# Router logits in narrow column tiles, rows of twelve groups turned by VectorE from a copy in DRAM

## The chip, the cores and the metric

One core of one Trainium2 chip. The metric is the device time of one execution in microseconds (us), the median of several runs. PE is TensorE, PEld its weight load, DVE is VectorE, ACT is ScalarE, POOL is GpSimd, SP is SyncE, whose queue issues most of the DMAs.

## The reference: what is computed

Three layers over 2304 tokens of 512 features, all in f32. Attention over 4 batches x 8 heads keeps the 32 largest scores of each row; a gated feed-forward layer (512 to 2048 to 512) follows; a router then gives each token to one of 8 experts (512 to 1024 to 512), weighted with a softmax probability. The change lies at the router's logits:

```python
xn = x / (np.linalg.norm(x, axis=-1, keepdims=True) + 1e-06)
en = expert_emb / (np.linalg.norm(expert_emb, axis=-1, keepdims=True) + 1e-06)
logits = xn @ en.T / tau
expert_idx = np.argmax(logits, axis=1)
```

## The kernel before, in words

The tokens form 18 groups of 128. A written-out loop of 76 steps handles 72 attention units; `step` (line 840) runs the names of one of four lists (FIRST, MID, THEN, ODD) in that order, so the program order on every engine is the order of the list. From step 21 on, even steps use THEN and odd steps ODD. An attention unit passes through five steps: scores (PE, `scores`), their copy (ACT, `take`), sorted halves and the top 32 (DVE, `pairs` and `select`), mask (ACT, POOL), exponent (ACT), scaling (POOL), nine transposes (PE, `turned`, line 521), and `values` (PE, line 539).

Two groups at a time go through the feed-forward layer (`push_group`), as eight items of one step each: `s1` (24 matmuls, line 603), `gate` (ACT), `swish` (DVE), `large` (ACT), `small` (POOL), and one step later `s2` (12 matmuls, line 638). After the eighth item `out_y` copies each group's rows from PSUM to SBUF (`ysb`, line 649), stores them to `y_dram` (line 650), and calls `route`.

`route` appends work to the list `side`. Each step pops one entry of it, at the name `aside`. Before the change a group has two entries. `r1`: ACT squares the row and sums it into `ss_all` (line 666), PE transposes four blocks (line 669), ACT copies them out (line 671). `r2`: four f32 matmuls with the transposed row as the 128 x 128 weights and 8 columns of the embedding `ent` moving (line 677; an f32 matmul is two instructions in the trace), then a DVE copy into `l_all` (line 678). After groups 3, 7, 11 and 13, `choose` and `rank` (which expert, which place) follow in the same list. Pairs of groups 0-1 to 14-15 go this way, eight pairs; the last pair of groups 16-17 is handled behind the loop (lines 1130 to 1145), where its eight transposes stand at line 1133.

Behind the loop, `behind` (line 1060) pops the last entries of `side` at fixed places between the remaining feed-forward items; then come the experts, which gather rows from `y_dram`.

PSUM banks of `bank()` alternate between two; `turned`, `r1` and `r2` share them. `ps_sc`, the bank pair of the scores, has one buffer: the scores of the next unit wait until DVE's `pairs` has read the last. The SBUF pool `stg` has three buffers of 4 KB a partition; the weights' preparation uses it up to step 20, `ysb` after that.

Of the kernel before, what the change touches and what calls it, by code (L numbers as in the profile page):

```python
# [8 lines left out]
F32 = mybir.dt.float32  # L9
# [4 lines left out]
AF = mybir.ActivationFunctionType  # L14
ALU = mybir.AluOpType
AX = mybir.AxisListType
# [4 lines left out]
DM, FF = 512, 2048  # L21
E, F2 = 8, 1024
# [7 lines left out]

TURNS = (0, 1, 2, 3, 4, 6, 7, 5)
ACROSS = (2, 3)
NEG = -3.0e38
BIG = 2.0 ** 100
NUNIT = 72
# [24 lines left out]
def fused_kernel(tc: tile.TileContext, *args):  # L60

    nc = tc.nc
    y_dram = tc.dram_tile([NT + 1, DM], F32, name="y_dram")
    g_dram = tc.dram_tile([NT + 128, 1], F32, name="g_dram")
    tbl = tc.dram_tile([E * STRIDE, 2], I32, name="tbl")

    lo_dram = [tc.dram_tile([8, 128, 1024], F32, name=f"lo_dram{n}") for n in range(2)]
    with ExitStack() as held:  # L70
        pools = [held.enter_context(tc.tile_pool(name=n, bufs=b, **kw)) for n, b, kw in
                 (("const", 1, {}), ("sm", 4, {}), ("fs", 1, {}), ("ps_a", 1, {"space": PSUM}))]
        flag = pools[0].tile([1, 2], I32, name="flag")
        consts = {}
        over_ = layers(tc, *args, y_dram, g_dram, tbl, lo_dram, flag, pools, consts)
        rare = nc.values_load(flag[0:1, 1:2], min_val=0, max_val=NT + 1)  # L76
        with tc.If(rare > 0):
            over_()
            again = nc.values_load(flag[0:1, 0:1], min_val=0, max_val=1)
            with tc.If(again > 0):  # L80
                layers(tc, *args, y_dram, g_dram, tbl, lo_dram, None, pools, consts)()


class Held:
# [7 lines left out]
        return self.tiles[name]  # L92


def layers(tc: tile.TileContext, qt, kt, v, w_in, w_out, embt, tau, w1, w2, out, y_dram, g_dram, tbl, lo_dram, flag, pools, consts):
    nc = tc.nc
    exact = flag is None

    const = Held(pools[0], consts)
    sm, fs, ps_a = pools[1:]  # L100
    ident = const.tile([128, 128], F32, name="ident")
    half = const.tile([128, 1], F32, name="half")
    iota8 = const.tile([128, 8], F32, name="iota8")
    ebase = const.tile([128, 8], F32, name="ebase")
    ones = const.tile([128, 128], BF16, name="ones")
    tri = const.tile([128, 128], BF16, name="tri")
    ids = const.tile([128, NG, 2], I32, name="ids")
    ent = const.tile([128, 4, E], F32, name="ent")
    picks = const.tile([128, NG, E], BF16, name="picks")
    before = const.tile([128, NG + 1, E], BF16, name="before")  # L110
    rev8 = const.tile([128, 8], F32, name="rev8")
# [2 lines left out]
    l_all = const.tile([128, NG, E], F32, name="l_all")  # L114
    ss_all = const.tile([128, NG], F32, name="ss_all")
# [4 lines left out]
    st = ExitStack()  # L120
# [4 lines left out]
    mp = st.enter_context(tc.tile_pool(name="mp", bufs=2))  # L125
    lop = st.enter_context(tc.tile_pool(name="lop", bufs=2))
    stg = st.enter_context(tc.tile_pool(name="stg", bufs=3))
# [8 lines left out]
    def bank():  # L136
        turn[1] ^= 1
        return bank_t[turn[1]]

    def half_a():  # L140
        turn[0] ^= 1
        return bank_a[:, turn[0], :]
# [11 lines left out]
    emb = {}  # L154

    def embed(part):

        if part == 0:
            emb["et"] = fs.tile([128, 4, E], F32, tag="df", name="et")
            nc.sync.dma_start(out=emb["et"], in_=embt.rearrange("(k p) e -> p k e", p=128))  # L160
            emb["tb"] = fs.tile([128, 1], F32, tag="gt", name="tb")
            nc.sync.dma_start(out=emb["tb"], in_=tau.rearrange("(o t) -> o t", o=1).broadcast_to([128, 1]))
        elif part == 1:
            emb["ones"] = mp.tile([128, DM], F32, tag="wf", name="onesf", bufs=4)[:, :128]
            nc.gpsimd.memset(emb["ones"], 1.0)
            emb["sq"] = fs.tile([128, 4, E], F32, tag="tmp", name="sq")
            nc.scalar.activation(emb["sq"], emb["et"], AF.Square)
        elif part == 2:
            onesf, sq = emb["ones"], emb["sq"]
            emb["pe"] = pe = half_a()  # L170
            for k in range(4):
                nc.tensor.matmul(pe[:, :E], onesf, sq[:, k, :], start=(k == 0), stop=(k == 3))
        elif part == 3:
            emb["nr"] = fs.tile([128, E], F32, tag="nrm", name="nr")
            nc.scalar.activation(emb["nr"], emb["pe"][:, :E], AF.Sqrt)
        else:
            nr = emb["nr"]
            nc.vector.tensor_scalar(nr, nr, 1e-6, emb["tb"][:, 0:1], op0=ALU.add, op1=ALU.mult)
            nc.vector.reciprocal(nr, nr)
            nc.vector.tensor_tensor(ent, emb["et"], nr.unsqueeze(1).broadcast_to([128, 4, E]), op=ALU.mult)  # L180
# [24 lines left out]
    for q in range(8):  # L205
        c = slice(256 * q, 256 * q + 256)
# [250 lines left out]
    def select(i, r):  # L457
# [13 lines left out]
        if r < TOPK // 8 - 1:  # L471
            for n in range(2):
                nc.vector.match_replace(dst[:, n, :w], A[:, n, 8 * r:8 * r + 8], src[:, n, :w], NEG)

# [101 lines left out]
    side = deque()  # L576
    step = [0]

    done_groups, scored, chosen = [0], [0], [0]
# [4 lines left out]
    def push_group(X, gs):  # L584
# [3 lines left out]
        state = {}  # L588
# [56 lines left out]

        def out_y(o):
            final = gs[o] >= NG - 2
            t = late["xg"].tile([128, DM], F32, tag="xg", name="ysl") if final else stg.tile([128, DM], F32, tag="st", name="ysb")
            nc.scalar.copy(t, state["y"][o])
            nc.sync.dma_start(out=y_dram[128 * gs[o]:128 * gs[o] + 128, :], in_=t)  # L650
            if final:
                finals.append((t, gs[o]))
            else:
                route(t, gs[o])

        for q in range(8):
            moe.append((q, s1, gate, swish, large, small, s2, len(gs)))
# [2 lines left out]

    def route(ysb, g):
        state = {}

        def r1():
            sq = mp.tile([128, DM], F32, tag="wf", name="sqy", bufs=4)
            nc.scalar.activation(sq, ysb, AF.Square, accum_out=ss_all[:, g:g + 1])
            pp = bank()
            for k in range(4):
                nc.tensor.transpose(pp[:, 128 * k:128 * k + 128], ysb[:, 128 * k:128 * k + 128], ident)
            yt = mp.tile([128, DM], F32, tag="ug", name="yt", bufs=1).rearrange("p (k n) -> p k n", k=4)  # L670
            nc.scalar.copy(yt, pp.rearrange("p (k n) -> p k n", k=4))
            state["yt"] = yt

        def r2():
            p2 = bank()[:, :E]
            for k in range(4):
                nc.tensor.matmul(p2, state["yt"][:, k, :], ent[:, k, :], start=(k == 0), stop=(k == 3))
            nc.vector.tensor_copy(l_all[:, g, :], p2)
            scored[0] += 1

        side.extend((r1, r2))
        if g in (3, 7, 11, 13):
            side.extend((choose, rank))

    open_ = deque()
# [55 lines left out]
    late = {}  # L741
# [150 lines left out]
    if True:  # L892
# [17 lines left out]
        def hidden(r, f, c0, c1, half=None):  # L910
            xh_, xl_ = tok[r]
            h1, l1 = ws1[r]
            if r not in hs:
                hs[r] = [hp.tile([128, 8, CAPS[0]], F32R, tag=t, name=t) for t in ("hh", "hl")]
            if half != 1:
                xt_[f] = late["ph"].tile([128, 512], F32, tag="ph", name="ph2")[:, :c1 - c0]
            ph = xt_[f]
            for k in ((0, 1), (2, 3), (0, 1, 2, 3))[2 if half is None else half]:
                for n, (l, x) in enumerate(((h1, xh_), (h1, xl_), (l1, xh_))):
                    nc.tensor.matmul(ph, l[:, k, 128 * f:128 * f + 128], x[:, k, c0:c1], start=(k == 0 and n == 0), stop=(k == 3 and n == 2))  # L920
# [37 lines left out]
        def columns(r, d):  # L958
# [3 lines left out]
            if d == 0:  # L962
                across[r] = gp.tile([128, 4, CAPS[ACROSS[0]]], F32, tag="ot", name="ot", bufs=1)
            po = po_.tile([128, DM], F32, tag="po", name="po4")[:, :m]
# [135 lines left out]
        with tc.manual_schedule():  # L1100
# [29 lines left out]
            for o, (t, g) in enumerate(finals):  # L1130
                pp = px.tile([128, 4, 128], F32, tag="px", name="pxt")
                for k in range(4):
                    nc.tensor.transpose(pp[:, k, :], t[:, 128 * k:128 * k + 128], ident)
                yts.append(gp.tile([128, 4, 128], F32, tag="ob", name="ytl"))
                nc.scalar.copy(yts[o], pp)
                hidden(0, 1, *C, o)
            hidden_out(0, 0, *C)
            p2 = half_a()
# [47 lines left out]
            def leave(r, b):  # L1186
                rows_out(r, b)
                if ahead_:
                    gates(*ahead_.popleft())

            back = deque()
            for r, then, nn in zip(TURNS, TURNS[1:] + (None,), TURNS[2:] + (None, None)):
# [16 lines left out]
                if nn is not None:  # L1209
                    load2(nn)  # L1210
                    for x in bl[nn]:
                        get(nn, x)
                for n, b in enumerate(b2 if r not in ACROSS else range(4)):
                    if r in ACROSS:
                        columns(r, n)
# [4 lines left out]
                    if n == 0 and then is not None:  # L1220
                        for k in range(4):
                            split_1(then, k)
                        if nn is not None:
                            load1(nn)
                    if r not in ACROSS:
                        leave(r, b)
                if r in ACROSS:
                    back.extend((r, b) for b in b2)
# [95 lines left out]
```

## Time and profile before

| | us |
|---|---|
| median of 3 runs | 1027.08 (1026.25 to 1028.41) |
| the profiled execution | 1029.51 |
| its span, first to last instruction | 1027.8 |
| PE busy in the span | 953.9 |
| DVE busy | 760.3 |
| ACT busy | 715.1 |
| POOL busy | 632.0 |

The profile is of one execution, 2.4 us above the median. Busy time of PE includes the fill of the pipeline, so a busy share of 100% doesn't by itself mean matmuls back to back; distances between starts do. In a view of groups a row has the line, engine, operation, tiles, shapes and count, then the busy time and the mean duration of one in ns, then the idle time before and what ended it.

### The profile page before, as it was taken

The numbers are of one execution on the slowest core, as the hardware profiler recorded it, in microseconds if no ns is written. First come the engines' busy times: TensorE is split into PE (matmuls) and PEld (weight loads), VectorE is DVE, ScalarE is ACT, GpSimd is POOL, SyncE is SP. The second block draws the span as 40 slices with busy tenths as digits, with TensorE's granted clock in tenths as the row PEclk, the third lists the DMA queues.
The fourth block names the chain that finished last, engine by engine and source line by source line (L and its number), as shares of the span: only waits on it lengthen the run. The fifth ranks groups of instructions, "written<-read, shape, count | busy, mean of one in ns | idle before, by whom it ended". The sixth has DMA issues, their size and how long they took to land. (4 is left out here: it accounts for less than half of the span.)

```text
span 1027.8 us, 20958 instructions
## 1 busy us (share of the span) xinstructions
PE 953.9 (93%) x7268; PEld 842.0 (82%) x7268; DVE 760.3 (74%) x2349; ACT 715.1 (70%) x1445; POOL 632.0 (61%) x786
## 2 busy tenths in 40 slices
PE   3665787999999999999999999999999999999997
PEld 1443566889999899999999988789898888999996
DVE  7999999998988988988988888881234454555550
ACT  4899798897888787788787786775234453455551
POOL 4789899877778877778877665765232253034320
PEclk9956799999999999999999999999999999999999
DMA  5555678644445653456654275575586466445610
GB/s 199 178 158 176 223 238 270 216 159 141 140 140 173 206 177 118 114 173 179 183 168 143 81 246 198 138 240 197 164 254 218 130 228 216 169 147 195 253 75 22
DMA packets 85905, 180.96 MB, mean 176 GB/s; under 512 B 16157, under 2 KB 30640, under 8 KB 85791
## 3 DMA queue, kind: packets, MB, share of 16 engines
q1 hardware_dynamic: 81231, 169.68, 51.4%
q0 software_dynamic: 4416, 9.80, 3.0%
q8 instruction: 59, 0.97, 0.4%
q14 instruction: 55, 0.45, 0.1%
q10 hardware_dynamic: 144, 0.07, 0.0%
HBM read 157.41 MB, written 18.89 MB: 172 GB/s over the span
## 5 line engine op out<-in xcount | busy, mean ns | idle before, releaser
L488 POOL TENSOR_TENSOR s<-s,z 128x576 f32<-128x576 f32 x144 | 189.4, 1317 | 63.1 <-ACT z L484 62.6
L603 PE MATMUL bank_h<-xh,vh 128*128 128x256 f32 x576 | 170.7, 296 | 0.0
L603 PE MATMUL bank_h<-xh,lo 128*128 128x256 f32 x576 | 162.9, 283 | 0.3 <-DMA lo<-lo_dram 0.3
L603 PE MATMUL bank_h<-xl,vh 128*128 128x256 f32 x576 | 163.0, 283 | 0.0
L470 DVE MAX8 A<-left 128x8 f32<-128x288 f32 (+1 forms) x288 | 159.6, 595 | 0.0
L521 PE MATMUL bank_t<-ident,s 128*128 128x128 f32 x648 | 108.2, 290 | 30.4 <-ACT pt L526 19.7
L526 ACT COPY pt<-bank_t 128x384 f32<-128x384 f32 x216 | 102.1, 482 | 37.0 <-PE bank_t L521 35.9
L521 PEld LDWEIGHTS bank_t<-ident,s 128*128 128x128 f32 x648 | 81.6, 148 | 52.7 <-ACT pt L526 22.8
L622 POOL TENSOR_TENSOR gl<-u,gh 128x512 fp32r<-128x512 f32 x72 | 92.9, 1290 | 46.9 <-ACT gh L619 46.9
L442 ACT COPY s<-ps_sc 128x576 f32<-128x576 f32 x143 | 92.1, 644 | 38.2 <-PE ps_sc L431 14.0
L638 PE MATMUL y<-wh,gh 128*128 128x512 f32 x288 | 117.7, 409 | 0.0
L484 ACT ACTIVATE z<-s,nb 128x576 bf16<-128x576 f32 x144 | 112.7, 782 | 4.4 <-POOL nb L478 4.4
L494 ACT ACTIVATE s<-s,nb 128x576 f32<-128x576 f32 x144 | 113.4, 789 | 0.6 <-POOL s L488 0.6
L638 PE MATMUL y<-wh,gl 128*128 128x512 f32 x288 | 113.3, 394 | 0.3 <-POOL gl L622 0.3
L638 PE MATMUL y<-lo,gh 128*128 128x512 f32 x288 | 113.3, 393 | 0.0
L603 PEld LDWEIGHTS bank_h<-xl,vh 128*128 128x128 f32 x576 | 110.2, 191 | 0.3
L603 PEld LDWEIGHTS bank_h<-xh,lo 128*128 128x128 f32 x576 | 109.9, 191 | 0.5 <-DMA lo<-lo_dram 0.5
L603 PEld LDWEIGHTS bank_h<-xh,vh 128*128 128x128 f32 x576 | 110.1, 191 | 0.3
L994 POOL DMA_INDIRECT out_dram<-ob,idt x21 | 24.9, 1185 | 135.2 <-ACT ob L987 104.0
L539 PE MATMUL bank_a<-pt,vt 128*64 128x128 f32 (+1 forms) x1600 | 95.6, 279 | 0.6 <-ACT pt L526 0.6
L510 POOL TENSOR_SCALAR s<-s,sums 128x576 f32<-128x576 f32 x112 | 82.4, 746 | 21.0 <-DVE sums L501 19.9
L926 DVE SCALAR_TENSOR_TENSOR hl<-ph,hh 128x256 fp32r<-128x256 f32 (+5 forms) x72 | 31.7, 440 | 85.2 <-ACT hh L925 82.4
(258 smaller groups left out, 2659.0 us busy)
## 6 DMA issues: line engine op xcount, KB each, us to landing
lo<-lo_dram SPq DMA_DIRECT2D x144, 512.0 KB
a<-in_moe_w_dram SPq DMA_DIRECT2D x64, 512.0 KB
vt<-in_v_dram SPq DMA_DIRECT2D x28, 320.0 KB
w<-in_moe_w_in_dram SPq DMA_DIRECT2D x16, 512.0 KB
w<-in_moe_w_out_dram SPq DMA_DIRECT2D x16, 512.0 KB
lo_dram<-wf SPq DMA_DIRECT2D x32, 256.0 KB
qraw<-in_q_dram SPq DMA_DIRECT2D x48, 128.0 KB
krs<-in_k_dram SPq DMA_DIRECT2D x16, 288.0 KB
```

Of the source, the lines that this page charges most:

```text
L442: nc.scalar.copy(sbuf[i % NS][:, :, HS * g:HS * g + HS], ps_[i][:, :, :HS])
L470: nc.vector.max(A[:, n, 8 * r:8 * r + 8], src[:, n, :w])
L484: nc.scalar.activation(zb_[n], tile_of(i, n), AF.Relu, bias=sel[i][1][:, n, 1:2], scale=-BIG)
L488: nc.gpsimd.tensor_tensor(s, s, zb_[n], op=ALU.subtract)
L494: nc.scalar.activation(s, s, AF.Exp, bias=sel[i][1][:, n, 0:1], scale=SCALE, accum_out=sums[i][:, n:n + 1])
L510: nc.gpsimd.tensor_scalar(x, x, rv[:, n:n + 1], 1.0, op0=ALU.mult, op1=ALU.mult)
L521: nc.tensor.transpose(pp[:, 128 * k:128 * k + 128], e[:, 128 * (3 * c + k):128 * (3 * c + k) + 128], ident)
L526: nc.scalar.copy(pts[i][:, 3 * c:3 * c + 3, :].rearrange("p k n -> p (k n)"), tb_.pop((i, c))[:, :384])
L539: nc.tensor.matmul(av[64 * n:64 * n + 64, c0:c1], vt[:, k, 64 * n:64 * n + 64], pt[:, k + 5 * n if k < 4 else 4, c0:c1], start=(o == 0), s ...
L603: nc.tensor.matmul(ph[:, a, :], w, x[:, k, :], start=(k == 0 and n == 0), stop=(k == 3 and n == 2))
L622: nc.gpsimd.tensor_tensor(state[q][1], state.pop((q, "u")).rearrange("p (a n) -> p a n", a=2), state[q][0].bitcast(F32), op=ALU.subtract)
L638: nc.tensor.matmul(state["y"][o], x[:, a, c], w, start=(f == 0 and n == 0), stop=(f == 15 and n == 2))
```

## The change

- `out_y` copies both groups of a pair into one tile `ysb` of 128 x 2 x 512 and calls `route` once for a pair. The store to `y_dram` becomes one DMA of 512 KB; for the first six pairs (groups 0 to 11, `TURNED = 12`) it is an entry of `side`, a step later; for groups 12 to 15 it is issued at once.
- The first six pairs also store the same rows to `yq_dram`, features cut into four quarters, and an entry later load them back as `ya`, where partition 32n + c holds quarter n of tokens 4c to 4c+3. Two entries `r1` then have DVE turn 32 x 32 blocks of `ya` into `yt`, one group each; no PE transposes and no ACT copy.
- For groups 12 to 17 PE still transposes, with every fourth feature read as a block (a step of 16 bytes).
- The embedding is loaded as `(p k)` in place of `(k p)`, so that block k holds features 4p + k. It lies beside the identity in one tile `both`.
- `r2` has four f32 matmuls for a pair: 32 columns of `both` are the weights, 256 tokens move, and block k writes PSUM partitions 32k to 32k+31. ACT copies the 128 x 256 result to `lt`. A new entry `r3` transposes `lt` back in two blocks, and DVE adds the four partial sums of each logit into `l_all`.
- The square is written over `ysb` in place of a scratch tile. `choose` and `rank` follow the same pairs of groups.

```diff
-    ident = const.tile([128, 128], F32, name="ident")
+    both = const.tile([128, 4 * E + 128], F32, name="both")
+    ident, ent = both[:, 4 * E:], both[:, :4 * E].rearrange("p (k e) -> p k e", k=4)
...
-            nc.sync.dma_start(out=emb["et"], in_=embt.rearrange("(k p) e -> p k e", p=128))
+            nc.sync.dma_start(out=emb["et"], in_=embt.rearrange("(p k) e -> p k e", k=4))
...
+            if o == 0:
+                state["t"] = stg.tile([128, 2, DM], F32, tag="st", name="ysb")
+            nc.scalar.copy(state["t"][:, o, :], state["y"][o])
+            if o == 1:
+                route(state["t"], gs[0])
...
-        def r1():
-            sq = mp.tile([128, DM], F32, tag="wf", name="sqy", bufs=4)
-            nc.scalar.activation(sq, ysb, AF.Square, accum_out=ss_all[:, g:g + 1])
-            pp = bank()
+        inside = g < TURNED
+
+        def store():
+            nc.sync.dma_start(out=y_dram[128 * g:128 * g + 256, :].rearrange("(o p) x -> p o x", p=128), in_=ysb)
+            if inside:
+                nc.sync.dma_start(out=yq_dram.rearrange("m p x -> p m x"), in_=ysb.rearrange("p o (n x) -> p (o n) x", n=4))
+
+        def load():
+            state["ya"] = stg.tile([128, 2, DM], F32, tag="st", name="ya")
+            nc.sync.dma_start(out=state["ya"], in_=yq_dram.rearrange("(o n) (c i) x -> (n c) o (i x)", o=2, i=4))
+
+        def r1(o):
+            if o == 0:
+                state["yt"] = stg.tile([128, 4, 256], F32, tag="st", name="yt")
+            yt = state["yt"][:, :, 128 * o:128 * o + 128]
+            if inside:
+                nc.vector.transpose(yt.rearrange("p k (i c) -> p i k c", i=4), state["ya"][:, o, :].rearrange("p (i r k) -> p i k r", i=4, k=4))
+            else:
+                pp = bank()
+                for k in range(4):
+                    nc.tensor.transpose(pp[:, 128 * k:128 * k + 128], ysb[:, o, :].rearrange("p (x k) -> p k x", k=4)[:, k], ident)
+                nc.scalar.copy(yt, pp.rearrange("p (k n) -> p k n", k=4))
+            nc.scalar.activation(ysb[:, o, :], ysb[:, o, :], AF.Square, accum_out=ss_all[:, g + o:g + o + 1])
+
+        def r2():
+            pq = bank()[:, :256]
             for k in range(4):
-                nc.tensor.transpose(pp[:, 128 * k:128 * k + 128], ysb[:, 128 * k:128 * k + 128], ident)
-            yt = mp.tile([128, DM], F32, tag="ug", name="yt", bufs=1).rearrange("p (k n) -> p k n", k=4)
-            nc.scalar.copy(yt, pp.rearrange("p (k n) -> p k n", k=4))
-            state["yt"] = yt
-
-        def r2():
-            p2 = bank()[:, :E]
-            for k in range(4):
-                nc.tensor.matmul(p2, state["yt"][:, k, :], ent[:, k, :], start=(k == 0), stop=(k == 3))
-            nc.vector.tensor_copy(l_all[:, g, :], p2)
-            scored[0] += 1
-
-        side.extend((r1, r2))
-        if g in (3, 7, 11, 13):
+                nc.tensor.matmul(pq[32 * k:32 * k + 32, :], both[:, E * k:E * k + 32], state["yt"][:, k, :], start=True, stop=True)
+            state["lt"] = lt = mp.tile([128, DM], F32, tag="ug", name="lt", bufs=1)[:, :256]
+            if inside:
+                nc.scalar.copy(lt.rearrange("p (o c i) -> p o i c", o=2, i=4), pq.rearrange("p (o i c) -> p o i c", o=2, i=4))
+            else:
+                nc.scalar.copy(lt, pq)
+
+        def r3():
+            p2 = bank()[:, :256]
+            for o in range(2):
+                nc.tensor.transpose(p2[:, 128 * o:128 * o + 128], state["lt"][:, 128 * o:128 * o + 128], ident)
+            nc.vector.tensor_reduce(l_all[:, g:g + 2, :], p2.rearrange("p (o k e) -> p o e k", o=2, k=4)[:, :, :E, :], axis=AX.X, op=ALU.add)
+            scored[0] += 2
+
+        if g >= 12:
+            store()
+        else:
+            side.extend((store, load) if inside else (store,))
+        side.extend((lambda: r1(0), lambda: r1(1), r2, r3))
+        if g in (2, 6, 10, 12):
             side.extend((choose, rank))
...
-                    nc.tensor.transpose(pp[:, k, :], t[:, 128 * k:128 * k + 128], ident)
+                    nc.tensor.transpose(pp[:, k, :], t.rearrange("p (x k) -> p k x", k=4)[:, k], ident)
```

## Rows read from the trace of the kernel before

**Rows 1.** The page, busy time of the engines and the granted clock in 40 slices.

```profile
PE 953.9 (93%) x7268; PEld 842.0 (82%) x7268; DVE 760.3 (74%) x2349; ACT 715.1 (70%) x1445; POOL 632.0 (61%) x786
...
PEclk9956799999999999999999999999999999999999
```

**Rows 2.** Busy us by stretch: PE, PEld, DVE, ACT, POOL; granted clock, DMA share, GB/s.

```profile
100.00:150.00 50.00, 38.00 (x274) 29.59 (x276) 49.05 (x150) 43.48 (x88) 44.17 (x45) 0.81 0.69 223
...
250.00:300.00 50.00, 50.00 (x411) 45.79 (x411) 44.02 (x152) 39.62 (x87) 35.61 (x52) 1.00 0.49 163
```

**Rows 3.** PE in order of time: start, duration; first matmul of line 603 in successive steps.

```profile
282.70 0.36 PE L603 MATMUL bank_h<-xh,vh 128*128 128x256 f32 x1
...
292.55 0.37 PE L603 MATMUL bank_h<-xh,vh 128*128 128x256 f32 x1
...
301.28 0.36 PE L603 MATMUL bank_h<-xh,vh 128*128 128x256 f32 x1
...
312.07 0.37 PE L603 MATMUL bank_h<-xh,vh 128*128 128x256 f32 x1
...
320.49 0.36 PE L603 MATMUL bank_h<-xh,vh 128*128 128x256 f32 x1
...
331.29 0.37 PE L603 MATMUL bank_h<-xh,vh 128*128 128x256 f32 x1
...
339.28 0.36 PE L603 MATMUL bank_h<-xh,vh 128*128 128x256 f32 x1
```

**Rows 4.** PE in order of time: one group's transposes, and its logits one step later.

```profile
297.51 0.60 PE L669 MATMUL bank_t<-ident,ysb 128*128 128x128 f32 x4
...
308.17 0.95 PE L677 MATMUL bank_t<-ent,yt 128*128 128x8 f32 x8
```

**Rows 5.** PE in order of time: matmuls on parts of the array, and their neighbours.

```profile
305.19 2.40 PE L539 MATMUL bank_a<-pt,vt 128*64 128x128 f32 x40
...
612.11 0.49 PE L521 MATMUL bank_t<-ident,s 128*128 128x128 f32 x3
612.53 0.71 PE L431 MATMUL ps_sc<-krs,qpl 64*64 64x288 f32 x8
613.18 0.55 PE L521 MATMUL bank_t<-ident,s 128*128 128x128 f32 x3
```

**Rows 6.** DVE in two steps without routing (THEN, ODD), and PE's next scores; idle time in brackets.

```profile
261.93 0.69 DVE L615 SCALAR_TENSOR_TENSOR u<-u,bank_h 128x512 f32<-128x512 f32 x1 [0.17 <-ACT u L611]
262.84 0.47 DVE L451 TENSOR_TENSOR ps_sc<-ps_sc,s 128x288 f32<-128x288 f32 x1 [0.22 <-ACT s L442]
...
271.73 0.17 DVE L501 RECIPROCAL sums<-sums 128x2 f32<-128x2 f32 x1 [0.97 <-POOL sums L498]
272.61 0.47 DVE L451 TENSOR_TENSOR ps_sc<-ps_sc,s 128x288 f32<-128x288 f32 x1 [0.71 <-ACT s L442]
...
274.51 0.45 DVE L455 TENSOR_TENSOR left<-ps_sc,left 128x288 f32<-128x288 f32 x1
...
276.47 0.38 PE L435 MATMUL ps_sc<-kst,qh 128*128 128x288 f32 x1
```

**Rows 7.** Groups by line and shape: busy us, mean ns of one, idle before.

```profile
L237 DVE TENSOR_SCALAR wf<-w 128x512 int32<-128x512 int32 x32 | 17.0, 532 | 5.3 <-DMA w<-in_moe_w_in_dram 5.3
L244 DVE SCALAR_TENSOR_TENSOR wf<-w,wf 128x512 int32<-128x512 int32 x32 | 29.6, 925 | 0.7
L671 ACT COPY yt<-bank_t 128x512 f32<-128x512 f32 x16 | 9.7, 603 | 0.0
L925 ACT ACTIVATE hh<-ph 128x256 fp32r<-128x256 f32 x32 | 12.2, 384 | 23.3 <-PE ph L920 21.6 <-issue 0.8
```

**Rows 8.** Waits of SP's queue; its issues in order of time; PE's first use of that load.

```profile
SPq L650 <- ACT ysb L649: 86.1, 9, 13.5
...
293.53 0.38 SPq L287 DMA_DIRECT2D lo<-lo_dram  x1
...
298.18 0.39 PE L638 MATMUL y<-lo,gh 128*128 128x512 f32 x1
```

More of the change, by code (lines that the diff above doesn't have):

```diff
@@ L32 @@
 ACROSS = (2, 3)
+TURNED = 12
 NEG = -3.0e38
@@ L67, in fused_kernel @@
     tbl = tc.dram_tile([E * STRIDE, 2], I32, name="tbl")
+    yq_dram = tc.dram_tile([8, 128, 128], F32, name="yq_dram")
     lo_dram = [tc.dram_tile([8, 128, 1024], F32, name=f"lo_dram{n}") for n in range(2)]
@@ L74, in fused_kernel @@
         consts = {}
-        over_ = layers(tc, *args, y_dram, g_dram, tbl, lo_dram, flag, pools, consts)
+        over_ = layers(tc, *args, y_dram, yq_dram, g_dram, tbl, lo_dram, flag, pools, consts)
         rare = nc.values_load(flag[0:1, 1:2], min_val=0, max_val=NT + 1)
@@ L80, in fused_kernel @@
             with tc.If(again > 0):
-                layers(tc, *args, y_dram, g_dram, tbl, lo_dram, None, pools, consts)()
+                layers(tc, *args, y_dram, yq_dram, g_dram, tbl, lo_dram, None, pools, consts)()
 class Held:
@@ L92, in tile, with layers @@
         return self.tiles[name]
-def layers(tc: tile.TileContext, qt, kt, v, w_in, w_out, embt, tau, w1, w2, out, y_dram, g_dram, tbl, lo_dram, flag, pools, consts):
+def layers(tc: tile.TileContext, qt, kt, v, w_in, w_out, embt, tau, w1, w2, out, y_dram, yq_dram, g_dram, tbl, lo_dram, flag, pools, consts):
     nc = tc.nc
@@ L107, in layers @@
     ids = const.tile([128, NG, 2], I32, name="ids")
-    ent = const.tile([128, 4, E], F32, name="ent")
     picks = const.tile([128, NG, E], BF16, name="picks")
@@ L647, in out_y @@
             final = gs[o] >= NG - 2
-            t = late["xg"].tile([128, DM], F32, tag="xg", name="ysl") if final else stg.tile([128, DM], F32, tag="st", name="ysb")
-            nc.scalar.copy(t, state["y"][o])
-            nc.sync.dma_start(out=y_dram[128 * gs[o]:128 * gs[o] + 128, :], in_=t)
             if final:
+                t = late["xg"].tile([128, DM], F32, tag="xg", name="ysl")
+                nc.scalar.copy(t, state["y"][o])
+                nc.sync.dma_start(out=y_dram[128 * gs[o]:128 * gs[o] + 128, :], in_=t)
                 finals.append((t, gs[o]))
-            else:
-                route(t, gs[o])
+                return
+            if o == 0:
[3 more added lines that the diff above has]
+                route(state["t"], gs[0])
         for q in range(8):
```

## The prediction

> **What bounds the kernel now.** I read the page first, then busy time by stretch, then starts on PE. On the page PE is busy 93% of the span, and the granted clock is at 9 tenths or more from the sixth slice on, about 130 us [rows 1]; between 250 and 300 us it is 1.00, the 2.4 GHz level [rows 2]. In that stretch PE is busy 50.00 of 50 us, beside 44.02 for DVE and 39.62 for ACT [rows 2]; the stretches up to 700 us look alike. A busy PE could still hide small waits, so I measured steps by PE's own starts. A THEN step without routing lasts 7.99 us (331.29 to 339.28), an ODD step without it 9.85 us (282.70 to 292.55). With routing the four steps of a pair last 8.73, 10.79, 8.42 and 10.80 us [rows 3]. The routing entries thus lengthen the steps by what they take on PE: a group's `r1` by 0.43 us (8.42 less 7.99) and its `r2` by 0.94 us (10.79 less 9.85). That is what a chain on one engine looks like: PE's own order of work sets the time, and what is taken from PE comes off the end as long as no other engine gets late. The first `r1` of a pair shows 0.74 us. Of that I count 0.31 as not its own: ACT copies the pair's rows out of PSUM there, before and after the change.
>
> **Removed from PE.** For a pair: two `r1` and two `r2`, 2 x 0.43 + 2 x 0.94 = 2.74 us. The rows agree with these lengths: four transposes are 0.11 us apart, and the eight logit instructions have 0.95 us from first start to last end although only 8 columns move [rows 4].
>
> **Added to PE, r2.** Eight instructions (two for each f32 matmul) of 256 columns, each on a quarter of the array's columns. A full-height f32 transpose of 128 columns takes 0.11 us, so a pass of 256 columns takes about 0.22. Nothing in the trace shows four tiles of 128 rows x 32 columns; the near rows are two. Line 431 runs eight instructions of 288 columns on four 64 x 64 tiles: the next instruction starts 0.65 us after the first, and 0.09 us is lost ahead (612.53 less 612.11 less 3 x 0.11), 0.74 in all [rows 5]. One after another at that pace eight would need 8 x 0.245 = 1.96 us; two rounds need 0.49, which leaves 0.25 for the two changes of tile shape. So four run side by side there. Line 539 has full height and 64 columns: 40 instructions of 128 columns in 2.40 us, 0.06 each, so two side by side. The cost here is thus 2 x 0.22 + 0.25 = 0.69 us with four side by side, 4 x 0.22 + 0.25 = 1.13 with two, 8 x 0.22 + 0.25 = 2.01 with none. I take 0.69: the tile count is that of line 431, and two full-height streams already ran at no loss.
>
> **Added to PE, r3.** Two transposes, 0.24 us. For groups 12 to 15 `r1` keeps its 0.43 us a group.
>
> **Sum on PE.** Six pairs: 2.74 - 0.69 - 0.24 = 1.81, times six 10.9 us. Two pairs: 2.74 - 0.86 - 0.69 - 0.24 = 0.95, times two 1.9 us. Together 12.8 us. The last pair's eight transposes and `choose` and `rank` keep their count and their parity of steps.
>
> **Added to DVE.** Twelve turns of 128 x 512. No row shows one. DVE's work on 128 x 512 in SBUF takes from 0.53 us (one input, read at a step of 8 bytes) to 0.93 us (two inputs) [rows 7]; I take 0.6 as the nearest, with one input, and keep up to several times that for the range, since a turn is another kind of operation. Away go two copies into `l_all` a pair, in comes one reduction of 64 elements; that about cancels. Where does 0.6 us go? In a THEN step DVE idles 0.17 + 0.22 us, in the ODD step 0.97 + 0.71 us [rows 6]. The two turns of a pair fall into one THEN and one ODD step, ahead of `inverse` and `pairs`: idle time of 2.07 us takes up 1.2. What queues behind a late turn is `pairs`, and for it the next scores on PE: DVE's last instruction of `pairs` ends at 274.96, PE's next scores start at 276.47 [rows 6], 1.5 us of lead. DVE can also run fuller: 49.05 of 50 us between 100 and 150 us, at an unsaturated PE [rows 2]. So the turns cost nothing up to (2.07 + 1.5) / 2 = 1.8 us each.
>
> The Trainium skill, VectorE: DVE Perf Modes, section "The three transpose paths", gives 311 ns for a 128 x 128 bf16 turn on VectorE; four times that is an estimate of 1.24 us for 128 x 512, if f32 goes at the same pace. No run here shows it. By it the sum stays the same, since 1.24 is still under the cover.
>
> **ACT.** A turned pair loses two copies of 0.60 us and gains one of 128 x 256, some 0.38 [rows 7]. ACT has 39.62 of 50 us busy [rows 2], so I count nothing.
>
> **SP and the DMAs.** SP is held for up to 13.5 us at the old row stores, 86.1 us in nine waits [rows 8]; with the store an entry later that wait shrinks, and loads go out earlier. None of it ends on PE, so I credit nothing. New is that `load` waits at SP for the copy in DRAM to land, with the `lo` and q loads queued behind it. A `lo` load of 512 KB issued at 293.53 was used without a wait at 298.18 [rows 8], so 512 KB land within 4.65 us, and an entry lasts 8 to 10 us. The same holds for `ya` ahead of the turn. 6 MB more traffic beside 163 GB/s at a DMA share of 0.49 [rows 2] costs nothing on PE; if it came late, each us over a step's length would go the way of a late turn.
>
> **A new wait, once.** For groups 14 and 15 the store is issued at once and the square overwrites `ysb`: ACT waits for the landing, with the copy of `yt` and `gate` queued behind it, and PE's `r2` waits for that copy. At most 4.65 us; PE has a whole first stage to do meanwhile, so I take 0.5 us. For groups 12 and 13 a step lies between.
>
> **Result.** 12.8 - 0.5 = 12.3 us. Against the profiled execution, 1029.51 us, that is 1017.2; it was 2.4 us above the median, and against the median, 1027.08, it is **1014.8 us**. Uncertain by itself: 1012 (the 0.31 us of the first `r1` goes too, 8 x 0.3) to 1017.
>
> **Rivals.**
> - *The narrow matmuls don't run four at a time*: the part "in narrow tiles" doesn't do what it says. Two at a time add 8 x 0.44 = 3.5 us: 1018.3. None add 8 x 1.32 = 10.6: 1025.4. For it: four full-height f32 streams appear nowhere. Against it: lines 431 and 539 lose nothing [rows 5]. Chance 0.12 and 0.05.
> - *Reads at a step of 16 bytes are slow on PE*: groups 12 to 17 keep 24 transposes, now with every fourth f32. At half pace they add 24 x 0.11 = 2.6 us: 1017.4. For it: PE's moving operands are dense everywhere before. Against it: at 0.11 us for 128 columns a transpose moves a column in 0.85 ns, which leaves time. Chance 0.12. The Trainium skill, SBUF — State Buffer, section "Door 1: The DMA port swizzle", says SBUF works in lines of 16 bytes and each access that crosses to a new line pays; by that rule these reads pay each time. No row here shows one.
> - *The turn is dearer than its cover, but less than the gain*: between 1.8 and 2.8 us each, a pair loses 2p - 3.57 us; at 2.3 us 6 x 1.03 = 6.2 us: 1021. Chance 0.12, since the price is the least known here.
> - *Slower than before, by the same place*: DVE's turn stands in order ahead of `inverse` and `pairs`. Above p = (3.57 + 2.05) / 2 = 2.8 us, where 2.05 is the gain for each turned pair (12.3 / 6), PE waits longer for the scores' bank than it has won. At 3.3 us: 6 x (6.6 - 3.57) = 18.2 us lost, 12.3 won: 1033. That would be 6.4 ns an element, beside 1.0 to 1.8 in the rows [rows 7]. Chance 0.07; in it I include a `ya` that lands late by as much, since it stops DVE at the same instruction.
>
> **How the numbers follow.** Forecast 0.52, the rivals 0.17, 0.12, 0.12 and 0.07. The range reaches from 1011.5 (everything hidden, some of ACT's 0.31 too) to 1021 (two at a time together with strided reads, or a turn of 2.3 us); without the serial case, half of the dear turns and the slower case it holds about 0.8. A measurement of this kernel can tell some 0.2% (2 us) from no change. Faster by more than that: 0.52 + 0.12 + 0.12 + 0.11 = 0.87; within it 0.06 (serial matmuls, the dear end of the turns); slower 0.07.
>
> **What would show it.** Right: steps at line 603 of 8.0 and 9.9 us where `store`, `load` and the turns stand, 8.7 and 10.1 us where `r2` and `r3` stand; the eight narrow instructions as two rounds of four starts. A turn on DVE near 0.6 us; idle time of DVE ahead of line 451 smaller by that. Wrong: PE idle at line 435 until DVE's `pairs`, DVE idle at the turn until `ya` lands, or the narrow instructions 0.2 us apart.

## The result and the profile after

The changed kernel takes 1016.89 us (median of 5 runs, 1015.7 to 1017.79) where the kernel before took 1027.3 beside it (1026.25 to 1028.51): a ratio of 0.989, with a 95% interval from 0.9872 to 0.9908. It is 10.4 us faster; the forecast was 12.3. The profiled execution took 1016.89 us, its span 1015.1.

From the page of the kernel after, busy time of the engines and the granted clock in 40 slices:

```profile
PE 940.5 (93%) x7172; PEld 825.0 (81%) x7172; DVE 769.4 (76%) x2353; ACT 714.1 (70%) x1441; POOL 631.7 (62%) x786
...
PEclk9965799999999999999999999999999999999999
```

Beside [rows 1]: PE has 13.4 us less to do and keeps its 93%; DVE has 9 more. The granted clock is nearly the same. So the run got shorter by about what PE no longer does, as a chain on PE should.

The span fell by 12.7 us, but its two ends take differing times from execution to execution. From here on a step is the stretch from PE's first matmul of line 605 (603 before) in one first stage `s1` to that in the next, counted from 0; step n (from 1 on) begins in step n + 13 of the written-out loop, and steps from 63 on stand behind that loop. In all traces of this study, step 8 begins between 205.6 and 210.8 us, and what follows the start of step 66 lasts 283.1 to 286.0 us. I therefore compare traces by the stretch from the start of step 8 to that of step 66, and call it the loop. Kernel before, PE in order of time (start, duration), with the start of step 23 between:

```profile
207.48 0.36 PE L603 MATMUL bank_h<-xh,vh 128*128 128x256 f32 x1
...
349.88 0.37 PE L603 MATMUL bank_h<-xh,vh 128*128 128x256 f32 x1
...
741.77 0.36 PE L603 MATMUL bank_h<-xh,vh 128*128 128x256 f32 x1
```

Kernel after, the same two, and between them the starts of steps 17 to 23, which enclose the six steps of a turned pair:

```profile
205.56 0.36 PE L605 MATMUL bank_h<-xh,vh 128*128 128x256 f32 x1
...
288.89 0.36 PE L605 MATMUL bank_h<-xh,vh 128*128 128x256 f32 x1
...
297.16 0.36 PE L605 MATMUL bank_h<-xh,vh 128*128 128x256 f32 x1
...
307.05 0.36 PE L605 MATMUL bank_h<-xh,vh 128*128 128x256 f32 x1
...
315.04 0.36 PE L605 MATMUL bank_h<-xh,vh 128*128 128x256 f32 x1
...
324.92 0.36 PE L605 MATMUL bank_h<-xh,vh 128*128 128x256 f32 x1
...
333.66 0.36 PE L605 MATMUL bank_h<-xh,vh 128*128 128x256 f32 x1
...
343.76 0.36 PE L605 MATMUL bank_h<-xh,vh 128*128 128x256 f32 x1
...
729.74 0.36 PE L605 MATMUL bank_h<-xh,vh 128*128 128x256 f32 x1
```

The loop lasts 534.29 us before and 524.17 after: 10.12 less. Step by step (steps 17 to 22, the differences of starts; before by [rows 3] and 349.88):

| | THEN | ODD | THEN | ODD | THEN | ODD |
|---|---|---|---|---|---|---|
| before, us | 8.73 | 10.79 | 8.42 | 10.80 | 7.99 | 10.60 |
| after, us | 8.27 | 9.89 | 7.99 | 9.88 | 8.74 | 10.10 |
| entry, before | `r1` | `r2` | `r1` | `r2` | `choose` | `rank` |
| entry, after | `store` | `load` | turn | turn | `r2` | `r3` |

The bare steps are 7.99 and 9.85 [rows 3]. The steps whose entry has no work for PE are back there, but for the first, which keeps 0.28 of the 0.31 us that the prediction put down to ACT's copy of the rows; `r2` adds 0.75 and `r3` 0.25. A turned pair gains 2.7 and pays 1.0. The 10.60 before holds `rank` and, for the larger part, a wait for a `lo` load (PE's weight loads: start, duration, and in brackets the idle time ahead and what ended it):

```profile
340.08 0.19 PEld L603 LDWEIGHTS bank_h<-xh,lo 128*128 128x128 f32 x1 [0.53 <-DMA lo<-lo_dram]
```

In after `rank` falls into step 24, which lasts 10.02 without such a wait.

### The profile page after: what moved, and what is told of

The parts are those of the page before. It is cut to its first block, busy times and chain, and to the rows that moved or that the text cites. A ratio compares the mean times of both kernels' runs of the same rounds, so it can differ in the third digit from the quotient of the medians.

```text
span 1015.1 us, 20760 instructions
## 1 busy us (share of the span) xinstructions
PE 940.5 (93%) x7172; PEld 825.0 (81%) x7172; DVE 769.4 (76%) x2353; ACT 714.1 (70%) x1441; POOL 631.7 (62%) x786
## 5 line engine op out<-in xcount | busy, mean ns | idle before, releaser
L523 PE MATMUL bank_t<-both,s 128*128 128x128 f32 x648 | 107.8, 290 | 29.5 <-ACT pt L528 17.3
L523 PEld LDWEIGHTS bank_t<-both,s 128*128 128x128 f32 x648 | 81.3, 148 | 51.7 <-ACT pt L528 22.8
L861 DVE TENSOR_TENSOR l<-a,h 128x1024 fp32r<-128x1024 f32 x64 | 76.8, 1234 | 24.2 <-ACT h L860 23.6
```

Source lines behind the costliest of these rows:

```text
L523: nc.tensor.transpose(pp[:, 128 * k:128 * k + 128], e[:, 128 * (3 * c + k):128 * (3 * c + k) + 128], ident)
L861: nc.vector.tensor_tensor(lo, x, hi.bitcast(F32), op=ALU.subtract)
```

## The experiments

"After" is the changed kernel. Ratios are to the kernel before in the same measurement, with a 95% interval; loops are compared with 534.29 before and 524.17 after.

**1. The changed kernel again.** In after, the loop holds a step of 11.03 us where 9.88 was due (step 36). PE waits there for a `lo` load:

```profile
461.76 0.19 PEld L605 LDWEIGHTS bank_h<-xh,lo 128*128 128x128 f32 x1 [0.86 <-DMA lo<-lo_dram]
```

> The changed kernel once more, beside the three that follow. 1016.9 us by the first measurement (1015.7 to 1017.8). In its trace two waits of TensorE for a lo load (0.86 us in one step near 461 us, 0.37 us near 663 us) stood that the kernel before did not have. Theory: these are chance, and another execution has them elsewhere or not at all. Rival: the change causes them at these places, and they come again at the same steps.

Measured: 1018.34 us, 0.9915 (0.9893 to 0.9937), loop 524.23, and step 36 again at 11.03. So the wait at this place belongs to the change; in the other kernels that keep the turns (experiments 5 and 6 left out) the step lasts 9.95 to 11.31. But it isn't true that the kernel before had none: its own wait of 0.53 us in step 22 is gone in after. The load goes out when SP has got past its own wait for POOL; on SP's queue of after:

```profile
454.88 1.11 SPq L359 DMA_DIRECT2D kst<-kraw  x2
456.08 0.54 SPq L289 DMA_DIRECT2D lo<-lo_dram  x1
```

PE got there 4.8 us after the issue (461.76 less 0.86 of wait) and the load took 5.7 to be there. Before, it was issued at 465.11 and used at 470.26 without a wait, so it took 5.15 at most. Why it takes longer now isn't settled.

**2 and 3. Each half of the change alone.**

```diff
-TURNED = 12
+TURNED = 0
```

> The narrow logits without VectorE's turns: TURNED is 0, so TensorE turns all groups, with weights read at a step of 16 bytes, and no copy in yq_dram. Theory, TensorE's order of work sets the time and its terms add: a pair gains 2.74 - 2 x 0.55 - 0.76 - 0.24 = 0.64 us, eight pairs 5.1, less the wait of the last pair (1.2): 3.9 us faster than before, 1023.4. Rival 1, VectorE's turns carry the whole gain: 1027. Rival 2, the narrow matmuls carry it: 1017.

Measured: 1023.67 us, 0.9956 (0.9939 to 0.9973), loop 528.47, 5.8 less than before. The other half, the turn on VectorE with `r2` as it was before, once for each group, and no `r3` (further lines of the edit are left out; the turn then writes `yt` in the tokens' own order):

```diff
-            for k in range(4):
-                nc.tensor.matmul(pq[32 * k:32 * k + 32, :], both[:, E * k:E * k + 32], state["yt"][:, k, :], ...)
+            for k in range(4):
+                nc.tensor.matmul(p2, state["yt"][:, k, 128 * o:128 * o + 128], ent[:, k, :], ...)
```

> VectorE's turns without the narrow logits: six pairs turned by VectorE from the copy in DRAM, but logits as before with 128 x 128 weights and 8 columns moving, one entry for each group and no r3. Theory, TensorE's terms add: a turned pair gains the two r1, 2 x 0.43 = 0.86 us, six pairs 5.2; the last pairs lose some 0.4 by the strided reads and 1.2 by the wait for the store: 3.6 us faster than before, 1023.7. Rival 1, the narrow matmuls carry the whole gain: 1027. Rival 2, the turns carry it: 1017.

Measured: 1024.23 us, 0.9966 (0.995 to 0.9983), loop 529.51, 4.8 less. 5.8 and 4.8 make 10.6, beside 10.1 with both: the two gains add to within 0.5 us, as they should if both come off the same engine's order of work. By the medians they are 4.0 and 3.4, beside 9.3 with both in the same measurement (1027.65 before, 1018.34), each uncertain by some 2 us.

**4. One narrow tile in place of four.** All four products go to the same 32 columns and are summed there.

```diff
-pq[32 * k:32 * k + 32, :] ... start=True, stop=True
+pq[:32, :]                ... start=(k == 0), stop=(k == 3)
```

> The changed kernel with the four narrow matmuls of r2 in one and the same 32 columns of the array, summed in PSUM, so that none can run beside another; r3 turns back 32 rows instead of 128 and copies in place of adding. Theory, the gain of r2 comes from four column tiles side by side: eight passes of 256 columns one after another, 8 x 0.22 + 0.25 = 2.0 us in place of 0.7, 1.3 us more for each of eight pairs: 10 us slower than the changed kernel, 1027. Rival, the gain comes from fewer instructions and weight loads alone: 1017.

Measured: 1029.13 us, 1.0008 (0.9991 to 1.0025), loop 535.82. The eight instructions in this kernel and the one behind them, PE in order of time (start, first start to last end):

```profile
335.18 1.91 PE L696 MATMUL bank_t<-yt,both 128*32 128x256 f32 x8
337.02 0.50 PE L640 MATMUL y<-wh,gh 128*128 128x512 f32 x1
```

and in after:

```profile
329.66 0.64 PE L696 MATMUL bank_t<-yt,both 128*32 128x256 f32 x8
330.23 0.50 PE L640 MATMUL y<-wh,gh 128*128 128x512 f32 x1
```

1.27 us more for each `r2`, and the step with it grows by as much (10.01 for 8.74). One by one, the eight start 0.22 to 0.24 us apart here; in after they start in two rounds of four, at 329.66 and 329.90, each round within 0.02 us. So the four tiles run side by side in after, and without that the change gains nothing.

**5 and 6. The turn twice and three times.**

```diff
-                nc.vector.transpose(yt..., state["ya"][:, o, :]...)
+                for _ in range(2):            # 3 in the second kernel
+                    nc.vector.transpose(yt..., state["ya"][:, o, :]...)
```

> The changed kernel with each turn of VectorE issued twice (the second writes the same again): 2.2 us ahead of inverse and pairs in place of 1.1. Theory of the prediction, a pair's two turns are covered by 3.57 us (2.07 idle and 1.5 of lead): 2 x 2.2 - 3.57 = 0.83 us a pair, six pairs 5 us: 1022. Rival, lateness is carried on into the next steps, where VectorE idles too, and TensorE waits less than that: 1017 to 1018.5.

> The same with each turn issued three times, 3.3 us in place of 1.1. Theory of the prediction: 2 x 3.3 - 3.57 = 3.03 us a pair, six pairs 18 us: 1035, slower than before. Rival, lateness is carried on: VectorE has some 7 us idle in the eight steps of a pair and needs 4.4 more, so only what the lead doesn't cover is lost, 0.5 to 1 us a pair: 1020 to 1023.

Measured: 1026.01 us, 0.9981 (0.9963 to 0.9998), loop 531.71; and 1047.44 us, 1.0177 (1.0138 to 1.0215), loop 553.45. Twice costs 7.5 us over after, which neither theory had; three times 29.3. Where it waits, with two turns, in order of time:

```profile
327.43 2.22 DVE L686 STREAM_TRANSPOSE yt<-ya 128x512 f32<-128x512 f32 x2
329.59 0.11 DVE L503 RECIPROCAL sums<-sums 128x2 f32<-128x2 f32 x1
...
329.80 1.46 POOL L512 TENSOR_SCALAR s<-s,sums 128x576 f32<-128x576 f32 x2 [1.85 <-DVE sums L503]
...
330.60 0.31 PEld L523 LDWEIGHTS bank_t<-both,s 128*128 128x128 f32 x3 [1.72 <-POOL s L512]
```

The chain runs from the turn over DVE's `inverse` to POOL's `scale` to PE's transposes at line 523, and not, as I had it, over `pairs` to the next scores. In after, `inverse` follows the single turn in the same way, POOL waits 0.70 us for it, and PE doesn't wait; DVE and POOL in order of time:

```profile
321.81 1.08 DVE L685 STREAM_TRANSPOSE yt<-ya 128x512 f32<-128x512 f32 x1
322.82 0.12 DVE L503 RECIPROCAL sums<-sums 128x2 f32<-128x2 f32 x1
...
323.04 1.48 POOL L512 TENSOR_SCALAR s<-s,sums 128x576 f32<-128x576 f32 x2 [0.70 <-DVE sums L503]
```

My path over `pairs` exists too, but comes second. With three turns PE waits at the scores until `pairs` has ended at 330.07, and then 3.10 us more at line 523 in the same step, 20 (the view puts the first wait down to PE, whose work had long been done):

```profile
329.62 0.45 DVE L457 TENSOR_TENSOR left<-ps_sc,left 128x288 f32<-128x288 f32 x1
330.13 0.19 PEld L437 LDWEIGHTS ps_sc<-kst,qh 128*128 128x128 f32 x1 [0.91 <-PE bank_h L605]
```

With three turns there is a further loss that stands at no wait. Behind the late step the granted clock falls in five of the six pairs from 1.00 to 0.50, the 1.2 GHz level, for 3.4 us, and the step in which that falls lasts some 1.5 us longer (10.27 for 8.75 in step 29). Its first 3.2 us; PE, PEld, DVE, ACT, POOL busy, granted clock, DMA share, GB/s:

```profile
416.78:420.00 3.22, 3.22 (x18) 3.22 (x16) 3.22 (x17) 1.91 (x4) 3.05 (x5) 0.50 0.00 0
```

PE had waited 3.02 us in the step before, until 416.44. In step 20, after a wait of 3.10 us, the clock stayed at 1.00 and step 21 lasted 8.76 us.

**7. The store at once.** The row stores of groups 0 to 11 go out where they did before, at the end of the step; an empty entry keeps the others in place.

```diff
-        if g >= 12:
-            store()
-        else:
-            side.extend((store, load) if inside else (store,))
+        store()
+        if g < 12:
+            side.extend((lambda: None, load))
```

> The changed kernel with the stores of rows issued at once for all groups, not as an entry a step later; an empty entry keeps all others at their steps. Theory: SP is held at the store for ScalarE's copy as in the kernel before, loads of lo go out later, but TensorE has no wait for them: 1016.9, no change. Rival: the later store is part of the gain, SP's hold makes lo loads late by some 0.4 us a pair and more: 1019 to 1023.

Measured: 1043.73 us, 1.0171 (1.0129 to 1.0213), loop 546.50: both expectations were far off. The steps after a pair (9, 17, 25, 33, 41, 49) last 13.11, 10.87, 13.65, 11.26, 12.93 and 11.12 us where 8.28 is due, 23 us together. Of these, 18.8 are PE's waits for a `lo` load (2.6 to 3.8 us a step). The rest is the clock again: in steps 9, 25 and 41 the granted clock falls to 0.50 for 3.4 us behind the wait, and these steps last 1.5 us more than 8.28 and their wait; the other three don't. SP's queue of this kernel, and PE's wait:

```profile
282.02 0.32 SPq L289 DMA_DIRECT2D lo<-lo_dram  x1
...
296.11 0.37 SPq L672 DMA_DIRECT2D y_dram<-ysb  x1
296.53 0.46 SPq L674 DMA_DIRECT2D yq_dram<-ysb  x1
297.09 1.02 SPq L289 DMA_DIRECT2D lo<-lo_dram  x1
...
303.19 0.19 PEld L640 LDWEIGHTS y<-lo,gh 128*128 128x128 f32 x1 [2.62 <-DMA lo<-lo_dram]
```

SP stands at the store from 282.3 to 296.1, until the rows are there; the next `lo` load queues behind it and lands too late. Before, SP stood there as well, but only the two stores of the rows themselves went ahead of the load, and it was there 4.65 us after its issue at the latest [rows 8]; here PE wants it 3.48 us after its issue (303.19 less 2.62 of wait, less 297.09), and it takes 6.1. In after the stores go out at 289.45 and 289.87, with the next `lo` load ahead of them, and hold up no load for which PE waits.

**8. The store at once, but behind the load.** As the last, but the closure `store` is kept in a list and called in `s2`, right after the next `lo` load is issued.

```diff
                 ahead_of(1, m0 + q + 1)
+                while pend:
+                    pend.pop()()
```

> The run e6_store_at_once cost 26 us, against what I expected. Its trace has SP held at the store from 282 to 296 us, the store's 1 MB and then a lo load issued at 297.09, for which TensorE waited 2.62 us. Here the stores are still issued at once, in the same step, but behind that lo load in SP's order. Theory 1, the order on SP's queue is the cause (the lo load waits for ScalarE's copy of rows that it has nothing to do with, and for the bytes ahead of it): 1017 to 1019, as the changed kernel. Theory 2, the bytes of both stores at this place are the cause, in whatever order: 1030 to 1044.

Measured: 1017.34 us, 0.9905 (0.9888 to 0.9922), loop 524.39. SP's queue:

```profile
276.97 3.38 SPq L289 DMA_DIRECT2D lo<-lo_dram  x2
...
291.09 0.37 SPq L674 DMA_DIRECT2D y_dram<-ysb  x1
291.51 0.46 SPq L676 DMA_DIRECT2D yq_dram<-ysb  x1
```

With that order changed, 22.1 of the loop's 22.3 us are back. The moment of the store is the same in all three kernels: it goes out 0.56 to 0.57 us into step 17, when ACT has copied the rows. So the cause in experiment 7 is the order on SP's queue, not the moment of the store or its traffic as such. What the order does has two parts that no run separates: the load is issued 0.57 us later in the step than before (1.55 for 0.98), and it has the copy's 512 KB ahead of it as well.

**9. The square of the last groups into a tile of its own.** In after PE waits once for a `lo` load behind such a store (step 57), and once for ACT, which waits for a landing (step 65):

```profile
663.01 0.19 PEld L640 LDWEIGHTS y<-lo,gh 128*128 128x128 f32 x1 [0.37 <-DMA lo<-lo_dram]
...
724.92 0.63 ACT L691 ACTIVATE ysb<-ysb 128x512 f32<-128x512 f32 x1 [2.56 <-DMA y_dram<-ysb]
...
726.17 0.16 PEld L696 LDWEIGHTS bank_t<-yt,both 128*32 128x32 f32 x8 [1.28 <-ACT yt L690]
```

```diff
-nc.scalar.activation(ysb[:, o, :], ysb[:, o, :], AF.Square, ...)
+sq = ysb[:, o, :] if inside else mp.tile([128, DM], F32, tag="wf", name="sqy", bufs=4)
+nc.scalar.activation(sq, ysb[:, o, :], AF.Square, ...)
```

> The changed kernel, but for groups 12 to 15 the square goes to a scratch tile as before, and not over the rows that the store still reads. Theory: ScalarE no longer waits 2.56 us for the store's landing, the copy of yt comes 2.5 us earlier, and TensorE's wait of 1.28 us ahead of the last pair's narrow matmuls goes: 1.2 us less than the changed kernel, 1015.7. Rival: another wait ends there (the gate, or the choice of experts behind), and the time stays at 1016.9.

Measured: 1017.96 us, 0.9906 (0.9883 to 0.9928), loop 523.63; step 65 lasts 8.15 us for 8.25. So the rival came true. The wait for the landing is gone, and another stands in its place:

```profile
729.34 0.19 PEld L640 LDWEIGHTS y<-lo,gh 128*128 128x128 f32 x1 [1.12 <-DMA lo<-lo_dram]
```

The `lo` load again, issued 0.48 us behind the store of the rows (724.62 after 724.14 on SP's queue).

**10 and 11. The last stores behind the load too.** Experiment 9, with the stores of groups 12 to 15 called in `s2` as in experiment 8.

```diff
         if g >= 12:
-            store()
+            pend.append(store)
```

> The changed kernel with the square of groups 12 to 15 in a scratch tile (as e7_scratch) and their stores behind the lo load in SP's order (as e8_behind_lo). In e7_scratch the wait for the store's landing had gone, but TensorE waited 1.12 us for a lo load instead, which stood behind the store. Theory: both waits go, step 57 is 0.2 to 0.3 us shorter and step 65 1.1 us: 1.3 us below the changed kernel, 1016 to 1017 beside 1018 in the same measurement. Rival: something else ends there again, no change.

> The kernel of e10_last_behind_lo once more, since its four executions agree within 0.4 us while those of the changed kernel spread over 3, and its loop is only 1.5 us shorter in the trace. Theory: 1.3 to 1.5 us below the changed kernel's 1017 to 1018 is its own, the rest of 1013.4 is chance of the first eight steps: 1015 to 1016.5 here, a ratio to the kernel before of 0.988. Rival: it is 1013.4 again, a ratio of 0.986.

Measured: 1013.36 us, 0.986 (0.9845 to 0.9876), loop 522.66; again on another chip 1017.18 us, 0.9893 (0.9871 to 0.9915), loop 522.88. Step 65 lasts 7.11 us for 8.25 in both, so 1.1 us of the loop are won for certain. Step 57 lasts 9.05 for 9.37 in both, but it lasts 9.04 and 9.05 in experiments 2 and 5 too, where the store stands ahead of the load. By the total of the second measurement this kernel isn't told apart from the changed one. The 1013.36 wasn't luck of the first steps, as I had expected: step 8 begins at 205.78 us in the first trace and at 206.00 in the second. The two differ behind the loop, 283.20 beside 284.99 us (285.35 in after); why isn't settled.

**12. Dense blocks.** The embeddings stand in another order, so that the turn reads four whole blocks of 32 features, not every fourth f32. For groups 12 to 17 ACT copies the rows into that order ahead of PE's transposes.

```diff
-state["ya"][:, o, :].rearrange("p (i r k) -> p i k r", i=4, k=4)
+state["ya"][:, o, :].rearrange("p (i k r) -> p i k r", i=4, k=4)
...
+nc.scalar.copy(tmp.rearrange("p (k n r) -> p n k r", k=4, n=4), ysb[:, o, :].rearrange("p (n k r) -> p n k r", n=4, k=4))
```

> The changed kernel with another order of features in a block (feature 128n + 32k + r on partition 32n + r), so that VectorE's turn reads 32 neighbours in place of every fourth; for groups 12 to 17 ScalarE first copies the rows into that order (six copies more, some 0.6 us each), so that TensorE's transposes load dense weights. Theory, a step of 16 bytes is what makes the turn 1.10 us and the weight load 212 ns: they fall to some 0.6 us and to 140 ns as in the kernel before. Rival, the turn takes 1.1 us whatever its order. The time stays within 1 us of the changed kernel by both, as the turns are covered and the last pairs' transposes cost some 0.1 us a group.

Measured: 1025.19 us, 0.9979 (0.9964 to 0.9994), loop 529.72. The instructions of one line each (count: shortest/median/longest ns, first and last start), in this kernel:

```profile
L686 DVE STREAM_TRANSPOSE yt<-ya x12: 692/702/716, 241.0 to 613.8; 128x512 f32<-128x512 f32 x12
...
L692 PEld LDWEIGHTS bank_t<-both,tmpy x16: 138/141/226, 663.2 to 729.2; 128*128 128x128 f32 x16
```

and in after:

```profile
L685 DVE STREAM_TRANSPOSE yt<-ya x12: 1078/1100/1129, 240.4 to 614.2; 128x512 f32<-128x512 f32 x12
...
L689 PEld LDWEIGHTS bank_t<-both,ysb x16: 195/212/220, 662.0 to 723.3; 128*128 128x128 f32 x16
```

The step of 16 bytes makes a turn 1.6 times and a weight load 1.5 times as long. That much I expected; that the time would stay within 1 us was wrong, as the added copies stand directly ahead of PE's transposes. The weight loads of that line (busy us, mean ns of one, idle before and what ended it):

```profile
L692 PEld LDWEIGHTS bank_t<-both,tmpy 128*128 128x128 f32 x16 | 2.0, 158 | 7.8 <-ACT tmpy L690 7.8
```

7.8 us of waiting for the copy, and steps 57, 58, 64 and 65 grow to 10.37, 12.66, 7.39 and 10.68 us. Step 65 also holds 3.4 us at a granted clock of 0.50, from 728.8 us on, after two of these waits. The turn's own 0.4 us a time gave nothing back, since it was covered already.

## Why the prediction was right, and where its steps were off

The time, 1016.89, lies 2.1 us above the forecast and inside its range. The mechanism held: PE's order of work sets the time, and four tiles run side by side.

- **The bound.** Right. PE's order of work sets the time in the loop: experiments 2, 3 and 4 each moved the steps by the length of the PE instructions that they changed.
- **Removed, 2.74 us a turned pair.** Measured 2.71 (38.74 less 36.03 over the first four steps). The 0.31 us left out for ACT's copy stayed, as it was counted: 0.28.
- **`r2`, 0.69, and `r3`, 0.24.** Measured 0.75 and 0.25. The count of four side by side, read from line 431 [rows 5], holds; experiment 4 is the case without it. The rival "not four at a time" falls. Six pairs gain 6 x (2.71 - 1.00) = 10.3 us; forecast 10.9.
- **The turn, 0.6.** Mis-sized: 1.10 us, since a turn at a 16-byte step is dearer than the one-input rows that I took [rows 7]. Without a step it is 0.70. It did not matter: the ODD step with a turn lasts 9.88, beside 9.85 without. From the 311 ns that the Trainium skill, VectorE: DVE Perf Modes, section "The three transpose paths", states for 128 x 128 in bf16, the prediction's estimate was 1.24 us; the strided turn is nearer to that than to my 0.6, the dense one is not.
- **Its cover, 3.57 us a pair.** Wrong place. The first to be late is `inverse`, and through it POOL and line 523 (experiment 5); `pairs` and the scores come second, with 0.9 us at three turns (experiment 6). In experiment 5 all of the loss stands in the ODD step with the pair's second turn. The cover is about 3.1 us a pair: two turns of 2.2 less 7.5 / 6, a mean over losses of 0.4 to 2.2 us. The gain would be gone near 2.3 us a turn (on a line through the loops of experiments 5 and 6), not 2.8. So the rival on the other side had the right engine and order, and was nearer than I put it. Above that the loss grows faster than my sum: 29.3 us at 3.3, where 6 x (6.6 - 3.1) makes 21. The other 8 us are the clock's, a term that my sum didn't have: five steps behind the late ones last 1.5 us longer, 7.7 together.
- **Two pairs at the end, 1.9 less 0.5.** Wrong: 0.35 in steps 57 to 60 (37.46 to 37.11 us) and -0.21 in steps 64 to 66 (20.89 to 21.10). Three terms were missing or too small. The strided weight loads: 0.505 us from a group's four transposes to the next line's start, beside 0.41 before, in three of the four groups, and 0.40 beside 0.355 in the fourth. The `lo` load behind the store: 0.37 us of wait at 663.01. The landing: 1.28 us on PE, where I took 0.5. The strided rival was thus partly right, but with the weight loads as its place, not the moving columns, and 0.05 to 0.1 us a group, not 0.44. The Trainium skill, SBUF — State Buffer, section "Door 1: The DMA port swizzle", has each access that crosses to a new 16-byte line pay; experiment 12 agrees (212 ns beside 141 for a weight load).
- **ACT, 0.38 us for the new copy.** Mis-sized: 0.64 us, as it writes at a step of 16 bytes. No wait of PE comes of it.
- **"None of it ends on PE", of SP and the DMAs.** Wrong in both directions. The kernel before did wait on PE for a `lo` load, 0.53 us in step 22, and that is gone; step 36 gives 1.15 us back at another. And the credit of nothing for the store a step later hid what hangs on it: 22 us of the loop, some 26 by the medians (experiments 7 and 8; the profiled execution of 7 was the shortest of its four). A store at once now puts 1 MB ahead of a load that PE wants 3.5 us after its issue.

The sum over the loop: 10.3 + 0.30 - 1.15 = 9.4 us, of 10.12 (of the last pairs' 0.14, a loss of 0.16 in step 66 lies behind the loop). The wait of step 22, gone, adds 0.58 (10.60 in step 22 to 10.02 in step 24, both with `rank`); the last 0.1 I didn't trace. Against the forecast's 12.3 the six pairs fell short by 0.6 us, the last two by 1.1 and step 36 by 1.15, and 0.6 came unforeseen.

## What to carry to other kernels

Where one engine's order of work is the bound, measure steps by its own starts: the difference between a step with an entry and one without it priced this change to within 0.1 us a step. When work moves to an engine with idle time, follow each result that is queued behind it to the bounding engine and take the shortest slack, not the slack that comes to mind first. On SP's queue, which issued in program order here, a store that waits for its data belonged behind the loads that were needed soon. And a wait can cost more than its length: where the granted clock fell behind one, the step lost another 1.5 us.

## What the runs showed of the hardware

A VectorE turn of 128 x 512 f32 took 1.10 us reading every fourth f32 and 0.70 reading dense. PE's weight loads of 128 x 128 f32 took 212 ns and 141 ns in the same two cases. ACT's copy of 128 x 256 from PSUM took 638 ns when it wrote at a step of 16 bytes, beside 377 dense. In after (by line and shape: busy us, mean ns of one, idle before):

```profile
L699 ACT COPY lt<-bank_t 128x256 f32<-128x256 f32 x6 | 3.8, 638 | 0.4 <-PE bank_t L696 0.2
```

and in experiment 2, where all groups take the dense path:

```profile
L701 ACT COPY lt<-bank_t 128x256 f32<-128x256 f32 x8 | 3.0, 377 | 0.0
```

So a step of 16 bytes cost on all three engines, on one of them in writing. Four f32 products on tiles of 128 rows by 32 columns ran side by side: 0.57 us from the first start to the next line's, beside 1.84 on one tile. In three of these kernels the granted clock fell from 1.00 to 0.50 for 3.4 us behind waits of PE's weight loads of 2.1 to 3.8 us, nine times in all, and cost its step some 1.5 us; behind other waits of 2.3 to 3.1 us it stayed.
